# Gated linear attention and a squared-ReLU FFN on one core: a hand-written order of all work items is replaced by another order

## The chip, the cores and the metric

The kernel runs on one NeuronCore of a Trainium2 chip. The metric is device time in microseconds of one execution of the program; a few executions are made, and their median is quoted. Everything that is said of single instructions comes from one further execution, which the hardware profiler recorded.

## The reference: what is computed

The inputs of the attention are q, k, v and a complex gate (a_re, a_im), each of shape 4 x 8 x 768 x 48 (batch, heads, sequence, head dimension), in float32. The two weights of the FFN, 384 x 2048 and 2048 x 384, are float64.

```python
mag = np.sqrt(a_re * a_re + a_im * a_im)
scale = np.minimum(mag, 0.999) / (mag + 1e-06)
a_re_n, a_im_n = (a_re * scale, a_im * scale)
for t in range(S):                              # S_re, S_im start at zero
    ar, ai = a_re_n[:, :, t, :, None], a_im_n[:, :, t, :, None]
    new_re = ar * S_re - ai * S_im
    new_im = ar * S_im + ai * S_re
    S_re, S_im = new_re + einsum('bhd,bhe->bhde', k[:, :, t], v[:, :, t]), new_im
    y[:, :, t] = einsum('bhd,bhde->bhe', q[:, :, t], S_re)
x = y.transpose(0, 2, 1, 3).reshape(3072, 384)
h = np.maximum(x @ w_in, 0.0)
out = (h * h @ w_out).astype(np.float32)
```

## The kernel before

**Tiling.** Each sequence of 768 steps is cut into 6 chunks of 128. Two chunks of two different sequences form a *group*, so there are 12 groups, each of 2 x 128 = 256 tokens. Groups 0 to 5 walk through the first two sequences, 6 to 11 through the other two. Inside a chunk the recurrence is turned into matrix products (scores, a mask, a product with the values); between chunks a state of 48 x 48 per head is carried. When a group's 256 tokens are there, the FFN is run on them.

**Work items.** The whole program is a string of tokens, `FRONT` (line 1162 on), which `follow` (line 1307) reads from left to right. A token is a letter, a group or block number, and a step; `work` (line 1273 on) names the function behind each letter. Each function issues its few instructions on the engines that it needs. The block runs under `tc.manual_schedule` for all five engines, so every engine executes its instructions in the order in which the tokens stand, and semaphores make it wait where data or a buffer is not there yet. Nothing else sets the order: moving a token moves its instructions on all of its engines, and nothing else.

The letters that matter here, with `g` a group:

- `l`, `i`: loads of the four inputs a_re, a_im, q, k into one single buffer `raw` (on SyncE's queue and, for the first three groups, partly on GpSimd's). `v`: loads of the values. `f`, `j`: the two parts of the load of a weight block, on SyncE and GpSimd (blocks 0 to 7 are of w_in, 8 to 15 of w_out; three buffers `words`). `U`, `S` (ScalarE), `D`, `A` (VectorE): decoding of float64 words into float32; after `A` a block can be used.
- `w`, `W`: the weights are read once more, in 32 pieces, and checked for range. `w` is the load into the one buffer `again` (on SyncE's queue), `W` two passes of ScalarE over it. As there is one buffer, a `w` waits until the `W` before it has been done.
- `p0.k`, `q0.k`, `p1.k`, `q1.k`, and `og.k` from group 2 on: the 31 steps that make a group's operands from the gates (p and q are the two chunks of groups 0 and 1, done apart). Steps 3, 7, 11, 13, 15 to 17, 19, 20 and 23 to 30 are VectorE's, step 21 (`last_heads`) is six transfers on SyncE's queue, the others are ScalarE's.
- `ag.k`, `bg.k`: the steps of the group's two chunks. 0 scores (TensorE), 1 and 3 transposes of the keys (TensorE), 2 and 4 their copies (ScalarE), 5 mask (VectorE), 6 products with the values (TensorE), 7 copy to the token tile x (ScalarE), 8 sums for the state (TensorE), 9 new state (VectorE). `gg` (that is `g0`, `g0.1`, `g1.0`, ...): two small transfers that fill the gaps of x.
- `F`, `H`: first product of the FFN (TensorE, into one of two PSUM buffers of the pool `ph`) and ReLU with square (ScalarE, two passes). A group has eight of each from group 2 on (`Fg.0` to `Fg.7`); for groups 0 and 1 they are per chunk (`F0.1.0` is half 1 of blocks, chunk 0).
- `T`, `E`: the second product of groups 0 and 1 and its eviction. From group 2 on the second product is computed by seven products `Z0` to `Z6` of half-size blocks instead of eight; `X`, `Y`, `Q` (VectorE) are the sums of halves of h that this needs, `R0` to `R6` (`outputs`, line 1132 on) evict and add. `Z1`, `Z3` and `Z5` go into one tile `o_ps` that takes a buffer of the same pool `ph` as the first product; `R1`, `R3` and `R5` read it. `Z0`, `Z2`, `Z4` and `Z6` take turns in another tile. `t0` to `t3` make sums of blocks of w_out. `s`: stores.
- `M`: masks and zeroed buffers at the start. `K`: the verdict on the ranges; it decides at the end whether a slow general path has to be run, which does not happen with these inputs.

From group 4 to group 10 the string repeats nearly the same pattern: eight `F` with their `H`, then `Z0` to `Z6` between the steps of the two chunks of the next group, with the next group's operand steps strewn in, and a pair `W`, `w` at eight to four places of each group, in which the next `w` stands directly behind the `W` that frees its buffer.

Of the kernel before, what the change touches and what calls it, by code (L numbers as in the profile page):

```python
# [426 lines left out]
def quotient_path(ctx, tc, feat, vtok, w_in, w_out, w1, w2, out, n_seq, count):  # L427
# [245 lines left out]
    def weights(i, step):  # L673
        if i in words_of:
# [457 lines left out]
    def outputs(i, r):  # L1132
# [30 lines left out]
        "l0.0.0 M4 M8 M6 l0.0.1 j1 j0 i0.1.0 i0.1.1 M0 p0.0 p0.2 p0.3 M7 p0.4 q0.0 p0.5 q0.3 "  # L1163
        "p0.7 q0.4 q0.5 q0.7 M2 M3 f1 p0.8 p0.9 p0.1 p0.10 p0.11 p0.12 q0.2 U1 q0.1 S1 q0.8 "
        "q0.9 f0 U0 q0.10 D1 p0.15 p0.23 p0.24 p0.25 D0 p0.16 A1 p0.22 S0 f2 l0.1.1 l0.1.0 "
        "p0.26 q0.11 p0.27 j3 j2 j4 p0.13 q0.6 p0.17 A0 f3 f4 v0.0 p0.6 M1 p0.14 v0.1 l1.2.0 M5 "
        "p0.18 p0.19 D2 q0.12 q0.15 p0.28 p0.20 q0.22 U2 S2 f5 A2 U4 S4 p0.29 a0.3 a0.4 q0.23 "
        "D4 p0.30 a0.1 a0.2 U3 S3 q0.24 A4 q0.25 D3 q0.16 q0.26 q0.13 q0.27 A3 q0.17 p0.21 j6 "
        "j5 j7 f6 i1.2.0 a0.8 a0.0 a0.5 a0.6 q0.14 q0.18 U5 U6 a0.7 S5 i1.2.1 D6 q0.19 q0.28 "
        "q0.20 D5 p1.0 S6 p1.3 p1.4 p1.6 q0.29 q0.30 p1.5 g0.0 l1.2.1 f7 F0.0.0 A6 p1.7 A5 a0.9 "  # L1170
        "p1.2 p1.1 p1.9 p1.8 U7 p1.10 q1.0 b0.3 p1.11 D7 p1.12 b0.4 q0.21 f8 b0.0 f9 p1.15 q1.3 "
        "p1.23 S7 b0.1 A7 p1.24 b0.5 p1.22 b0.2 H0.0.0 p1.25 D8 p1.16 F0.1.0 f10 b0.8 b0.6 U8 "
        "H0.1.0 b0.7 S8 q1.4 F0.3.0 p1.13 p1.26 q1.1 U9 H0.3.0 p1.14 p1.27 A8 p1.17 p1.18 D9 "
        "p1.19 p1.28 p1.20 p1.29 p1.30 F0.2.0 T0.0.0 g0.1 F0.3.1 H0.2.0 S9 q1.2 H0.3.1 q1.5 U10 "
# [12 lines left out]
        "H1.2.1 H1.3.1 o3.15 o3.23 o3.24 b2.5 o3.25 o3.16 T1.0.1 a2.3 T1.1.1 T1.2.1 a2.4 b2.6 "
        "a2.8 b2.7 s1.0 g2 T1.3.1 T1.4.1 T1.5.1 T1.6.1 F2.7 F2.0 o3.13 o3.14 a2.9 o3.26 o3.27 "
        "o3.17 o3.18 o3.19 o3.28 o3.20 o3.29 o3.30 H2.7 s0.0 l4 H2.0 b2.3 T1.7.1 F2.1 b2.4 o4.0 "
        "H2.1 v3 o3.21 F2.2 o4.3 o4.2 E1.1 H2.2 o4.4 o4.5 o4.7 o4.8 F2.3 b2.1 F2.5 H2.5 o4.9 "  # L1190
        "b2.2 a3.0 X2.1 Y2.1 a3.5 F2.6 b2.8 a3.6 b2.9 o4.1 H2.3 X2.3 o4.10 a3.7 F2.4 a3.1 a3.2 "
        "b3.0 a3.3 Z2.0 H2.6 H2.4 t1 Y2.3 o4.11 o4.12 a3.4 b3.5 X2.0 a3.8 b3.6 Z2.1 Y2.0 o4.15 "
        "X2.2 Q2.1 Y2.2 Z2.3 a3.9 t2 t3 o4.23 o4.24 Q2.3 b3.7 g3 s1.1 F3.1 o4.22 R2.0 H3.1 R2.3 "
        "Q2.0 o4.25 Q2.2 Z2.2 b3.3 F3.4 o4.6 W0 R2.2 Z2.4 Z2.5 b3.4 H3.4 F3.5 o4.16 R2.1 o4.13 "
        "o4.14 o4.26 o4.27 o4.17 R2.5 v4 l5 w1 o4.18 H3.5 R2.4 o4.19 o4.28 F3.2 b3.1 F3.0 b3.2 "
        "H3.0 X3.0 o4.20 o4.29 o4.30 Z2.6 b3.8 b3.9 R2.6 H3.2 o5.6 F3.6 o4.21 X3.1 v5 s2.1 s2.0 "
        "o5.1 Y3.1 Y3.0 a4.1 F3.3 H3.6 X3.2 o5.2 Y3.2 F3.7 H3.3 a4.2 o5.0 a4.0 o5.3 H3.7 X3.3 "
        "o5.4 a4.3 Z3.0 a4.4 a4.5 o5.5 Y3.3 o5.7 a4.8 W1 w2 R3.0 a4.6 a4.9 o5.10 Z3.1 a4.7 o5.8 "
        "o5.9 Z3.2 R3.1 Q3.2 Q3.1 Q3.0 Q3.3 o5.11 b4.0 R3.2 b4.1 b4.5 o5.12 Z3.3 o5.22 o5.15 "
        "o5.23 o5.24 o5.25 b4.2 b4.6 W2 w3 R3.3 b4.3 b4.7 Z3.4 b4.4 g4 o5.13 b4.8 R3.4 o5.14 "  # L1200
        "Z3.5 v6 b4.9 l6 o5.16 o5.26 o5.27 W3 w4 F4.0 Z3.6 H4.0 R3.5 o5.17 F4.4 R3.6 o5.18 s3.0 "
        "o5.19 s3.1 F4.1 H4.4 F4.5 H4.1 X4.0 o5.20 o5.28 o5.29 o5.30 W4 w5 F4.2 H4.5 o6.6 F4.6 "
        "H4.2 X4.1 o5.21 Y4.1 o6.1 Y4.0 F4.3 H4.6 X4.2 o6.2 F4.7 Y4.2 H4.3 o6.0 a5.0 o6.3 H4.7 "
        "X4.3 o6.4 Z4.0 o6.5 a5.5 Y4.3 o6.7 a5.6 W5 w6 R4.0 Z4.1 a5.7 o6.10 o6.8 Z4.2 R4.1 Q4.2 "
        "o6.9 Q4.1 Q4.0 Q4.3 o6.11 b5.0 R4.2 Z4.3 b5.5 o6.12 o6.22 o6.15 o6.23 o6.24 o6.25 b5.6 "
        "W6 w7 R4.3 Z4.4 b5.7 v7 g5 o6.13 Z4.5 R4.4 o6.14 o6.16 o6.26 o6.27 Z4.6 l7 W7 w8 F5.0 "
        "R4.5 R4.6 o6.17 F5.4 H5.0 o6.18 o6.19 F5.1 H5.4 s4.0 s4.1 F5.5 H5.1 X5.0 o6.20 o6.28 "
        "o6.29 o6.30 W8 w9 F5.2 H5.5 o7.6 F5.6 X5.1 o6.21 H5.2 Y5.1 Y5.0 o7.1 a6.1 F5.3 H5.6 "
        "X5.2 o7.2 F5.7 Y5.2 H5.3 a6.2 a6.0 H5.7 X5.3 o7.0 a6.3 Z5.0 a6.5 a6.4 Y5.3 o7.3 a6.8 "
        "W9 w10 R5.0 o7.4 a6.6 a6.9 o7.5 Z5.1 a6.7 o7.7 o7.10 Z5.2 R5.1 Q5.2 o7.8 Q5.1 Q5.0 "  # L1210
        "Q5.3 o7.9 b6.0 o7.11 R5.2 b6.1 Z5.3 b6.2 b6.5 o7.12 b6.3 Z5.4 b6.4 o7.15 o7.23 o7.24 "
        "o7.25 W10 w11 R5.3 o7.22 b6.6 b6.8 b6.7 g6 R5.4 Z5.5 o7.13 v8 Z5.6 b6.9 o7.14 R5.5 "
        "o7.16 o7.26 o7.27 s5.0 W11 w12 F6.0 R5.6 l8 o7.17 F6.4 H6.0 F6.1 H6.4 X6.0 o7.18 Y6.0 "
        "s5.1 F6.5 o7.19 H6.1 W12 w13 F6.2 H6.5 X6.1 F6.6 H6.2 Y6.1 o7.20 o7.28 o7.29 o7.30 "
        "o8.6 F6.3 H6.6 o8.0 X6.2 o7.21 Y6.2 a7.1 o8.3 H6.3 F6.7 o8.1 Z6.0 H6.7 X6.3 o8.2 Y6.3 "
        "a7.0 W13 w14 R6.0 o8.4 a7.2 o8.5 a7.3 a7.5 Z6.1 a7.4 o8.7 Z6.2 R6.1 o8.10 Q6.2 Q6.1 "
        "o8.8 Q6.0 Q6.3 o8.9 a7.8 a7.6 a7.9 R6.2 Z6.3 a7.7 o8.11 b7.0 W14 w15 R6.3 o8.12 b7.1 "
        "b7.5 o8.22 Z6.4 o8.15 o8.23 o8.24 o8.25 b7.2 b7.6 b7.3 b7.7 Z6.5 b7.4 g7 R6.4 o8.13 "
        "b7.8 R6.5 o8.14 Z6.6 v9 b7.9 s6.0 l9 o8.16 o8.26 o8.27 W15 w16 F7.0 R6.6 F7.4 H7.0 "
        "o8.17 F7.1 H7.4 X7.0 o8.18 s6.1 Y7.0 F7.5 o8.19 H7.1 W16 w17 F7.2 H7.5 X7.1 F7.6 H7.2 "  # L1220
        "Y7.1 o8.20 o8.28 o8.29 o8.30 o9.6 F7.3 H7.6 o9.0 X7.2 o8.21 Y7.2 a8.1 o9.3 H7.3 F7.7 "
        "o9.1 Z7.0 H7.7 X7.3 o9.2 Y7.3 a8.0 W17 w18 R7.0 o9.4 a8.2 o9.5 a8.3 a8.5 Z7.1 a8.4 "
        "o9.7 Z7.2 R7.1 o9.10 Q7.2 Q7.1 o9.8 Q7.0 Q7.3 o9.9 a8.8 a8.6 a8.9 R7.2 Z7.3 a8.7 o9.11 "
        "b8.0 W18 w19 R7.3 o9.12 b8.1 b8.5 o9.22 Z7.4 o9.15 o9.23 o9.24 o9.25 b8.2 b8.6 b8.3 "
        "b8.7 Z7.5 b8.4 g8 R7.4 o9.13 b8.8 R7.5 o9.14 Z7.6 v10 b8.9 s7.0 l10 o9.16 o9.26 o9.27 "
        "W19 w20 F8.0 R7.6 F8.4 H8.0 o9.17 F8.1 H8.4 X8.0 o9.18 s7.1 Y8.0 F8.5 o9.19 H8.1 W20 "
        "w21 F8.2 H8.5 X8.1 F8.6 H8.2 Y8.1 o9.20 o9.28 o9.29 o9.30 o10.6 F8.3 H8.6 o10.0 X8.2 "
        "o9.21 Y8.2 a9.1 o10.3 H8.3 F8.7 o10.1 Z8.0 H8.7 X8.3 o10.2 Y8.3 a9.0 W21 w22 R8.0 "
        "o10.4 a9.2 o10.5 a9.3 a9.5 Z8.1 a9.4 o10.7 Z8.2 R8.1 o10.10 Q8.2 Q8.1 o10.8 Q8.0 Q8.3 "
# [141 lines left out]
```

## Time and profile before

| | us |
|---|---|
| three executions | 688.64, 689.97, 691.25 (median 689.97) |
| profiled execution, its own time | 688.9 |
| its span, first to last instruction | 687.1 |
| TensorE (PE) busy | 624.4 |
| TensorE's weight loads (beside the matmuls) | 552.9 |
| VectorE (DVE) busy | 498.9 |
| ScalarE (ACT) busy | 423.7 |
| GpSimd (POOL) busy | 35.4 |
| moved by DMA | 60.37 MB |

The page first gives each engine's busy time, then the span in 40 slices of 17.2 us, one digit a slice, in tenths. A group of instructions is named by line, engine and operation; many VectorE instructions come from one helper and so bear its line, 482. A wait is put down to the instruction that ended it. A matmul's end in the trace is modelled, so the distance from one start to the next is the better measure of what a matmul costs.

Since every engine follows the tokens in order, the trace can be read token by token: the instructions of an engine, counted off, fall to the tokens of the string. Times such as "R2.1 at 228.2" in the prediction are read in this way, in us from the start of the span.

### The profile page before, as it was taken

The numbers are of one execution on the slowest core, as the hardware profiler recorded it, in microseconds if no ns is written. First come the engines' busy times: TensorE is split into PE (matmuls) and PEld (weight loads), VectorE is DVE, ScalarE is ACT, GpSimd is POOL, SyncE is SP. The second block draws the span as 40 slices with busy tenths as digits, with TensorE's granted clock in tenths as the row PEclk, the third lists the DMA queues.
The fourth block names the chain that finished last, engine by engine and source line by source line (L and its number), as shares of the span: only waits on it lengthen the run. The fifth ranks groups of instructions, "written<-read, shape, count | busy, mean of one in ns | idle before, by whom it ended". The sixth has DMA issues, their size and how long they took to land.

```text
span 687.1 us, 13164 instructions
## 1 busy us (share of the span) xinstructions
PE 624.4 (91%) x5147; PEld 552.9 (80%) x5147; DVE 498.9 (73%) x973; ACT 423.7 (62%) x822; POOL 35.4 (5%) x82
## 2 busy tenths in 40 slices
PE   0058999999999699999999999989999999999996
PEld 0047987776889589989989999879979879989896
DVE  7989899969678668967858868858957966862130
ACT  6758997575674276496496585495486577451330
POOL 5250030000000000000000000000000000000000
PEclk9999999999999899999999999999999999999999
DMA  8987582441701341741731730730731531121101
GB/s 190 180 170 199 134 191 75 74 80 34 135 2 42 72 94 43 141 96 48 150 75 37 151 85 28 160 73 25 141 78 43 128 86 48 52 57 36 30 2 28
DMA packets 49232, 60.37 MB, mean 88 GB/s; under 512 B 6792, under 2 KB 40072, under 8 KB 49160
## 3 DMA queue, kind: packets, MB, share of 16 engines
q1 hardware_dynamic: 46336, 53.78, 35.4%
q0 software_dynamic: 2336, 5.21, 4.0%
q8 instruction: 42, 0.69, 0.4%
q10 hardware_dynamic: 488, 0.44, 0.2%
q14 instruction: 30, 0.25, 0.1%
HBM read 48.76 MB, written 4.72 MB: 78 GB/s over the span
## 4 chain that ended last, share of the span: by engine, by line
PE 69%; DMA 11%; DVE 8%; ACT 6%; SPq 3%; issue 1%; ACTq 0%; DVEq 0%
PE o_ps L1128 26%; PE h_ps L1038 22%; DMA raw<-in_feat_dram 8%; PE a_ps L921 6%; PE y L947 3%; PE h_ps L1022 3%; PE y L913 3%; PE add L969 2%; PE tp L928 2%; PE o_ps L1058 2%; DVE qk L482 2%; DMA again<-in_moe_w_out_dram 2%; DMA last<-qk 1%; DVE pr L482 1%; SPq L517 1%
## 5 line engine op out<-in xcount | busy, mean ns | idle before, releaser
L1038 PE MATMUL h_ps<-x,w 128*128 128x256 f32 x960 | 214.8, 382 | 10.8 <-DVE o L1004 5.9
L1038 PEld LDWEIGHTS h_ps<-x,w 128*128 128x128 f32 x960 | 181.9, 191 | 37.3 <-ACT h L1045 6.5
L1128 PE MATMUL o_ps<-w,h 128*128 128x192 f32 x640 | 111.1, 328 | 0.0
L1128 PEld LDWEIGHTS o_ps<-w,h 128*128 128x128 f32 x640 | 103.7, 190 | 1.9 <-issue 0.9
L1045 ACT ACTIVATE h<-h_ps 128x512 f32<-128x512 f32 x80 | 47.7, 597 | 61.7 <-PE h_ps L1038 60.2
L482 DVE TENSOR_TENSOR pr<-ab 128x384 f32<-128x384 f32 (+3 forms) x196 | 70.1, 375 | 3.9
L482 DVE TENSOR_TENSOR mix<-h 128x256 f32<-128x256 f32 x40 | 16.9, 423 | 62.9 <-ACT h L1046 62.8
L1128 PE MATMUL o_ps<-w_sum,mix 128*128 128x192 f32 x320 | 55.7, 328 | 0.0
L1022 PEld LDWEIGHTS h_ps<-x,w 128*128 128x128 f32 x384 | 47.9, 205 | 7.5 <-ACT room L750 3.5
L482 DVE TENSOR_TENSOR ab<-pr 128x48 f32<-128x48 f32 (+3 forms) x210 | 49.9, 260 | 5.3
L1022 PE MATMUL h_ps<-x,w 128*128 128x128 f32 x384 | 48.9, 289 | 4.9 <-DMA x<-x 3.1
L1128 PEld LDWEIGHTS o_ps<-w_sum,mix 128*128 128x128 f32 x320 | 52.1, 190 | 1.0 <-DVE state L482 0.7
L482 DVE TENSOR_TENSOR a<-a_ps,mask 128x1024 f32<-128x1024 f32 x24 | 29.3, 1223 | 31.5 <-PE a_ps L921 31.5
L1046 ACT ACTIVATE h<-h 128x512 f32<-128x512 f32 x80 | 50.5, 631 | 2.6
L482 DVE TENSOR_TENSOR qk<-ab,qk 128x768 f32<-128x768 f32 (+1 forms) x56 | 46.1, 842 | 1.1
L1058 PE MATMUL o_ps<-w,h 128*128 128x384 f32 x128 | 44.8, 491 | 0.0
L1001 ACT ACTIVATE o<-o_ps 128x192 f32<-128x192 f32 (+1 forms) x44 | 15.2, 345 | 45.6 <-PE o_ps L1128 45.1
L735 ACT ACTIVATE qk<-raw 128x768 f32<-128x768 f32 (+1 forms) x28 | 37.2, 1337 | 7.9 <-DVE raw L482 7.5
L921 PE MATMUL a_ps<-qk 48*128 48x128 f32 x576 | 39.9, 287 | 0.0
L482 DVE TENSOR_TENSOR room<-ab,carry 128x1344 f32<-128x1344 f32 (+1 forms) x28 | 36.7, 1352 | 3.1 <-ACT carry L851 3.0
L921 PEld LDWEIGHTS a_ps<-qk 48*128 48x128 f32 x576 | 35.2, 193 | 4.4 <-issue 4.3
L735 ACT ACTIVATE room<-z 128x768 f32<-128x768 f32 (+1 forms) x28 | 35.5, 1362 | 4.0 <-DVE z L782 4.0
(105 smaller groups left out, 892.5 us busy)
## 6 DMA issues: line engine op xcount, KB each, us to landing
raw<-in_feat_dram SPq DMA_DIRECT2D x40, 288.0 KB
words<-in_moe_w_out_dram SPq DMA_DIRECT2D x8, 768.0 KB
again<-in_moe_w_in_dram SPq DMA_DIRECT2D x16, 384.0 KB
again<-in_moe_w_out_dram SPq DMA_DIRECT2D x16, 384.0 KB
vt<-in_vtok_dram SPq DMA_DIRECT2D x24, 192.0 KB
out_dram<-o SPq DMA_DIRECT2D x23, 192.0 KB
last<-qk SPq DMA_DIRECT2D x60, 64.5 KB
raw<-in_feat_dram SPq DMA_DIRECT2D x120, 32.0 KB
```

What stands on the lines that cost most here:

```text
L482: nc.vector.tensor_tensor(out=out, in0=in0, in1=in1, op=op)
L735: nc.scalar.activation(out=out.rearrange("p c j n -> p c n j"), func=AF.Copy, in_=in_.rearrange("p c (n j) -> p c n j", j=L), **kwargs)
L913: nc.tensor.matmul(ys[p_ % 2][crossed(hh, p_), p_ // 2], lhsT=states[b][1 - c_seq % 2][rows(hh), c, p_], rhs=operand(c, p_, rows(hh)), sta ...
L921: nc.tensor.matmul(ps[:, hh, p_], lhsT=operand(2 + c, p_, rows(hh)), rhs=operand(c, p_, rows(hh)), start=(c == RE), stop=(c == IM))
L947: nc.tensor.matmul(tiles["y"][p_ % 2][crossed(hh, p_), p_ // 2], lhsT=v[:, at:at + ROWS], rhs=tiles["am"][:, hh, p_], start=(first and p_ ...
L1001: nc.scalar.activation(out=out, in_=x, func=AF.Copy, scale=of_w2)
L1022: nc.tensor.matmul(ps[:, j], lhsT=w1_blocks[:, k, g, at:at + P], rhs=x_of[i][:, g, b * C:(b + 1) * C], start=(g == 0), stop=(g == NG - 1))
L1038: nc.tensor.matmul(ps[:, j], lhsT=w1_blocks[:, k, g, at:at + P], rhs=x_of[i][:, g], start=(g == 0), stop=(g == NG - 1))
L1045: nc.scalar.activation(out=h, in_=h_ps[i, f], func=AF.Relu, scale=of_w1)
L1046: nc.scalar.activation(out=h, in_=h, func=AF.Square)
L1058: nc.tensor.matmul(o_of[i, b], lhsT=tokens_of(i, f, b)[:, j], rhs=w2[:, k], start=(k == 0), stop=(k == NFB - 1))
L1128: nc.tensor.matmul(to, lhsT=x(k)[:, j], rhs=factor(z)[:, 2 * k + j], start=(z in (0, 1, 3) and k == j == 0), stop=(k == KH // 2 - 1 and j ...
```

## The change

Only the string `FRONT` is another, and `sum_weights` asks for two sums by `get`, so that `t3` can be placed ahead of `t1` and `t2`. No instruction is added, taken away or given another shape; the sums on every engine are the same. The tokens of one group are in another order, the tokens of neighbouring groups are interleaved differently, and the pieces of the second reading of the weights come in an irregular order (`w7`, `w6`, `w8`, `w4`, `w9`, ...), from group 6 on with the `w` often just a few tokens ahead of its `W`. The diff, cut to four stretches: the start, the stretch in which group 2's second product ends, one later group, and the end.

```diff
@@ sum_weights
-        x, y = ((half[0][1], half[0][0]), (half[1][1], w2_sums[0] if i else None),
-                (half[1][0], w2_sums[1] if i > 1 else None), (half[1][1], half[0][1]))[i]
+        x, y = ((half[0][1], half[0][0]), (half[1][1], w2_sums.get(0)),
+                (half[1][0], w2_sums.get(1)), (half[1][1], half[0][1]))[i]
...
@@ FRONT
-        "l0.0.0 M4 M8 M6 l0.0.1 j1 j0 i0.1.0 i0.1.1 M0 p0.0 p0.2 p0.3 M7 p0.4 q0.0 p0.5 q0.3 "
-        "p0.7 q0.4 q0.5 q0.7 M2 M3 f1 p0.8 p0.9 p0.1 p0.10 p0.11 p0.12 q0.2 U1 q0.1 S1 q0.8 "
-        "q0.9 f0 U0 q0.10 D1 p0.15 p0.23 p0.24 p0.25 D0 p0.16 A1 p0.22 S0 f2 l0.1.1 l0.1.0 "
-        "p0.26 q0.11 p0.27 j3 j2 j4 p0.13 q0.6 p0.17 A0 f3 f4 v0.0 p0.6 M1 p0.14 v0.1 l1.2.0 M5 "
-        "p0.18 p0.19 D2 q0.12 q0.15 p0.28 p0.20 q0.22 U2 S2 f5 A2 U4 S4 p0.29 a0.3 a0.4 q0.23 "
-        "D4 p0.30 a0.1 a0.2 U3 S3 q0.24 A4 q0.25 D3 q0.16 q0.26 q0.13 q0.27 A3 q0.17 p0.21 j6 "
...
-        "X2.2 Q2.1 Y2.2 Z2.3 a3.9 t2 t3 o4.23 o4.24 Q2.3 b3.7 g3 s1.1 F3.1 o4.22 R2.0 H3.1 R2.3 "
-        "Q2.0 o4.25 Q2.2 Z2.2 b3.3 F3.4 o4.6 W0 R2.2 Z2.4 Z2.5 b3.4 H3.4 F3.5 o4.16 R2.1 o4.13 "
-        "o4.14 o4.26 o4.27 o4.17 R2.5 v4 l5 w1 o4.18 H3.5 R2.4 o4.19 o4.28 F3.2 b3.1 F3.0 b3.2 "
...
-        "b7.8 R6.5 o8.14 Z6.6 v9 b7.9 s6.0 l9 o8.16 o8.26 o8.27 W15 w16 F7.0 R6.6 F7.4 H7.0 "
-        "o8.17 F7.1 H7.4 X7.0 o8.18 s6.1 Y7.0 F7.5 o8.19 H7.1 W16 w17 F7.2 H7.5 X7.1 F7.6 H7.2 "
...
-        "Q10.0 Q10.3 a11.6 R10.2 Z10.3 a11.7 b11.0 W30 w31 R10.3 Z10.4 b11.5 b11.6 R10.4 Z10.5 "
-        "b11.7 g11 Z10.6 R10.5 s10.0 W31 F11.0 R10.6 s10.1 F11.4 H11.0 F11.1 H11.4 X11.0 K0 "
-        "Y11.0 F11.5 K1 H11.1 F11.2 H11.5 X11.1 Y11.1 F11.6 H11.2 F11.3 H11.6 X11.2 K2 Y11.2 "
...
+        "M7 M8 l0.0.0 M4 M2 M3 l0.0.1 M0 M1 p0.0 p0.2 p0.3 p0.4 p0.5 p0.7 q0.0 M6 q0.3 p0.9 "
+        "p0.8 p0.1 q0.4 p0.10 q0.5 p0.11 l0.1.0 f0 q0.7 i0.1.1 j0 i0.1.0 j1 j2 p0.12 p0.22 q0.8 "
+        "q0.10 U0 q0.1 q0.9 q0.2 S0 f1 U1 S1 p0.15 p0.23 D0 p0.24 p0.13 p0.25 q0.11 p0.16 A0 "
+        "p0.26 D1 f2 l0.1.1 f3 p0.27 M5 A1 p0.17 q0.22 p0.6 q0.13 p0.14 q0.12 q0.15 U2 p0.18 "
+        "q0.14 S2 p0.19 q0.23 D2 l1.2.0 f4 i1.2.0 j4 j3 j5 q0.24 p0.28 q0.25 p0.20 q0.16 p0.29 "
+        "q0.26 p0.30 q0.27 q0.17 a0.3 p0.21 a0.4 q0.6 i1.2.1 a0.1 p1.6 U3 q0.18 A2 U4 a0.2 S3 "
...
+        "a3.4 o4.11 o4.12 R2.0 R2.3 b3.5 o4.22 Z2.2 a3.1 b3.6 R2.2 a3.2 b3.7 a3.8 Q2.0 o4.15 t2 "
+        "o4.23 Q2.1 Z2.5 Z2.4 o4.13 a3.9 R2.5 R2.1 g3 w1 F3.3 o4.14 b3.1 H3.3 F3.7 H3.7 b3.2 l5 "
+        "s2.0 F3.2 o4.24 o4.25 R2.4 o4.16 o4.26 o4.27 b3.3 b3.4 o4.17 o4.18 o4.19 o4.20 o4.28 "
...
+        "o9.26 Q7.1 R7.4 o9.14 Z7.5 o9.27 o9.17 R7.5 o9.18 o9.19 w20 v10 g8 W20 F8.5 F8.1 l10 "
+        "w16 H8.5 F8.3 H8.1 F8.4 Z7.6 o9.28 b8.9 o9.20 H8.3 o10.0 o10.3 o9.29 o9.30 o10.6 W16 "
...
+        "o11.30 b10.1 F10.5 H10.5 F10.1 b10.2 H10.1 b10.3 F10.7 H10.7 b10.4 F10.3 H10.3 X10.1 "
+        "Y10.1 o11.21 s9.1 w23 W23 w28 a11.0 Z10.0 R10.0 a11.5 X10.3 Y10.3 Z10.1 X10.2 X10.0 "
+        "Y10.2 a11.6 b10.8 a11.7 W28 R10.1 Y10.0 Z10.2 b10.9 b11.0 Q10.2 Z10.3 Q10.1 Q10.0 "
+        "Q10.3 b11.5 b11.6 w27 R10.2 W27 w26 W26 b11.7 R10.3 Z10.4 Z10.5 R10.4 R10.5 w24 g11 "
+        "F11.2 W24 w25 W25 H11.2 Z10.6 F11.0 H11.0 w30 F11.4 H11.4 F11.1 H11.1 R10.6 F11.3 "
...
```

## The prediction

> **What bounds the kernel now.** I read the page's slices first, then what TensorE waits for, then the stretches in which it stands still.
>
> ```profile
> span 687.1 us, 13164 instructions
> ...
> PE   0058999999999699999999999989999999999996
> ...
> DVE  7989899969678668967858868858957966862130
> ...
> PEclk9999999999999899999999999999999999999999
> ```
>
> From the fourth slice on TensorE is full, but for a dip in slice 14 and the last slice. VectorE is as full as TensorE up to about 140 us and slack behind that. So two things set the end: when TensorE's dense stretch begins, and what it loses inside.
>
> How much it loses, I get from what each piece costs when it runs dense. The chain of waits gives it, since there the pieces follow each other without a gap:
>
> ```profile
> 641.69 10.36 PE h_ps L1038 x48
> ...
> 662.73 18.21 PE o_ps L1128 x112
> ```
>
> That is 10.36 / 4 = 2.59 us an `F` and 18.21 / 7 = 2.60 a `Z`. With the other chain pieces: 80 F x 2.59 = 207.2, 70 Z x 2.60 = 182.0, 16 half F x 2.69 = 43.0, 32 T x 1.29 = 41.3, 24 scores x 1.99 = 47.8, 20 state products x 1.03 = 20.6, 24 value products x 1.02 = 24.5, 20 state sums x 1.07 = 21.4, 40 transposes x 0.33 = 13.2: 601.0 us of work in both kernels. The span has 687.1, so 86 us are lost. Counting off the matmuls' starts at these prices: 51 us are lost before 60 us, 8 from 60 to 220, 8 from 220 to 240, 12 from 240 to 640, and 6 after the last matmul at 680.9 (eviction and store, the same in both). A new order can win only from these.
>
> ```profile
> PE h_ps L1038 <- DVE o L1004: 5.9, 1, 5.9
> PE h_ps L1038 <- ACT h L1045: 4.9, 4, 1.7
> ```
>
> These are the waits inside the dense stretch that an order can cure. The first is this, on VectorE's and TensorE's timelines:
>
> ```profile
> 228.17 0.36 DVE L1004 SCALAR_TENSOR_TENSOR o<-o_ps,o 128x192 f32<-128x192 f32 x1 [6.40 <-PE o_ps L1128]
> ...
> 236.18 0.61 DVE L1004 SCALAR_TENSOR_TENSOR o<-o_ps,o 128x192 f32<-128x192 f32 x2
> ```
> ```profile
> 236.59 4.54 PE L1038 MATMUL h_ps<-x,w 128*128 128x256 f32 x12 [5.92 <-DVE o L1004]
> ```
>
> `R2.1` needs `Z2.1`, which ended at 212.2, but it began at 228.17, just when `Z2.5` ended: both write the one tile `o_ps`, `Z2.5` stands ahead of `R2.1`, and the wait is for the tile. VectorE stood 6.4 us, then did `o4.13` to `o4.17` (8 us), and only then `R2.5`. The tile's `ph` buffer was not free for `F3.2` until then.
>
> **The change part by part.**
>
> *Group 2's eviction.* The new order has `Z2.5 Z2.4 o4.13 a3.9 R2.5 R2.1`, so VectorE has nothing queued between the last product and the two adds that free the buffer. The next to need it is now `F3.7`. Is it in time? From the end of `a3.0` VectorE has 10.3 us to `b3.5`, which waits for `b3.0`, 10.7 us later on TensorE; from there 10.6 us of its own work (11.2 at the 5% that instruction gaps add) to the end of `R2.1`: 22.0 us. TensorE has 23.7 us of work from `a3.0` to `F3.7`. So 1.7 us to spare and no wait. The wait's price is more than its length:
>
> ```profile
> 232.00:236.00 4.00, 0.00 (x0) 0.00 (x0) 3.65 (x17) 0.73 (x1) 0.00 (x0) 0.65 0.49 115
> 236.00:240.00 4.00, 3.41 (x8) 2.79 (x9) 3.97 (x7) 1.96 (x7) 0.00 (x0) 0.50 1.07 172
> ```
>
> The clock column (third from the end) falls to 0.50 after the stop, and `F3.2` took 4.54 instead of 2.59. Gain 5.92 + 1.95 = 7.9; I take 7.5, as some small wait will come into this place.
>
> *The second reading of the weights.* Three of the four waits on ACT h have this form in the chain:
>
> ```profile
> 442.36 0.53 ACT h L1046
> 442.88 3.72 DMA again<-in_moe_w_out_dram
> 446.60 0.02 issue
> ```
>
> `W16` stands ahead of `H7.5` on ScalarE, its load was issued late (SyncE was busy with the ten microseconds of `l9`), and ScalarE stood; then both `ph` buffers were full and TensorE waited at `F7.6`, `F8.6`, `F9.6`: 1.7, 1.4 and 1.3 us, 4.4 in all. In the new order a load of this kind has 3 us and more of ScalarE work between it and its `W` in groups 5 to 9 (after `w16`: three `H`, `o10.0`, `o10.6`). `W13` alone has only 1, but no `F` is due behind it. So all 4.4 go.
>
> New is a chain at the end: `W28`, `W27`, `W26`, `W24`, `W25` stand nearly side by side on ScalarE, and with one buffer each load waits for the pass before. A cycle is 3.72 us from issue to data by the row above, and 1.38 for the pass (446.62 to 448.00): 5.1 us. `W28` can begin when `a11.7` is done, 4.6 us after `Z10.0`; four cycles and a pass later, at 26.4, `W25` ends, and the first half of `H11.2` at 27.0. TensorE has 27.0 us of work from `Z10.0` to `F11.4`, which needs that buffer: just in time. `R10.3`, queued behind `W26`, ends at 17.3 where `Z10.5` wants to start at 16.6: 0.7 late. Here the Trainium skill ("DMA: Bandwidth & Descriptors", section "Anatomy of one DMA — SWDGE (gpsimd) path") would have 2.0 us fixed plus bytes at 436 GB/s, 0.9 for these 384 KB, so a cycle of 4.3 and no stall at all. The page's fit is for another queue and the trace shows 3.5 to 3.9 at three places, so I keep the row. Bounds: 0 by the page, 4 if a cycle is 6 us. I take 1.
>
> *The irregular middle.* Groups 4 to 10 are dense in both orders. I compared, dependency by dependency, the work ahead of producer and consumer; most slacks are 0.5 to 3 us where the old pattern had more. `F8.6` has 1 us behind `W16`, `a5.0` about 1 behind its transfer `o5.21`. Bounds 0 to 6 for what such places lose; 2 taken.
>
> *The front.* The work that VectorE has to do before `F0.2.0` can start (up to `A5`) grows from 48.8 to 55.5 us, since the loads of q and k come ahead of the weights and chunk 1's steps ahead of the decoding. `A5` ended at 57.3, that is 8.5 behind its sum; at the same delay it would be at 64.0. The new order delays VectorE more: `q0.11` now waits for `q0.1`, `q0.9`, `q0.2`, which stand behind `U0` on ScalarE, and `q0.19` for `q0.18` behind `U3`, whose load `j3` is behind `i1.2.0` on GpSimd's queue; about 2.5 together. So `F0.2.0` at 66.5. Then `b0.8`, `b0.6`, `F0.0.0`, `F0.3.0` to 76.7, `F0.3.1` waits 0.9 for `H0.0.0` on ScalarE, and `F0.1.1` starts at 80.3. Before it started at 78.9 with `T0.0.0` (1.3) done as well, so 77.6 for the same work: 2.7 lost. The first scores, at 45 us before, come later too (their transfer `p0.21` waits for `p0.30`, 35.2 before, 41 now), but `F0.1.0` at about 60 isn't held by them alone. One rule speaks against this part: the Trainium skill ("TensorE: Matmul & The Clock Gate", "Part 1: The HAM clock gate") has the clock halved after an idle window of 3.4 us, until a busy one has passed, as the two windows above show it. TensorE has a gap ahead of `F0.2.0`. By the rule alone I would add 1.7 us; but `F0.0.0` took 5.46 us for its 24 matmuls before (53.1 to 58.6, twice the price), so the first `F` runs slow in both, 60 to 65.3, and the gap is then 1.2: nothing added. Bounds -2 (no added delay on VectorE) to +9.
>
> *Sum*: 2.7 - 7.5 - 4.4 + 1 + 2 = -6.2. The span of 687.1 becomes 680.9. The profiled execution took 688.9, 1.8 more than its span, and lies 1.1 under the median of 689.97; I apply the difference to the median: **683.8 us**.
>
> **Rivals.** *The front slips (slower).* VectorE is full to 140 us, and the plan behind has its weights decoded just in time (`T0.7.0` wants `A15` within a microsecond). If `j3`, behind `i1.2.0` on GpSimd's queue, lands not at about 39 but at 50, ScalarE stands at `U3`, which all of chunk 1's steps follow, and the front loses 10 in place of 2.7. It decides from a front loss of 8.9 on. For it: the DMA share is 0.87 to 0.96 up to 40 us; against it: fewer weights are in flight by then. Time 690 + 1 = 691 at that price, 694 with 2 to 4 us of lost slack behind it.
>
> *The reloads and tight slacks eat it (no change).* A cycle of 6 us puts 4 us on the end, and tight places lose 4 instead of 2: -6.2 + 3 + 2 = -1.2, 688.8. Against it: no load was seen to take over 3.9.
>
> *More than I say (faster still).* VectorE's added delay in the front doesn't occur (0 in place of 2.7) and the middle loses nothing: -6.2 - 2.7 - 2 = -10.9, 679.1.
>
> *It only moves the wait.* `R2.5` is freed, but another late evict stops TensorE by 5 us: -1.2 again, counted with the second.
>
> **How the numbers follow.** Forecast 0.42, faster still 0.18, no change 0.21, front slips 0.19. A difference of 0.5%, 3.4 us, is about what a measurement of this kernel can tell from none. Of the forecast's 0.42, within 3 us of 683.8, some 0.36 lies below 686.5; with the 0.18: faster 0.55. Same: 0.06 + the no-change case's 0.19 = 0.25. Slower: 0.20. The range goes from 676 (the faster case less 3) to 695 (the front at its bound); the forecast's own range is 681 to 687.
>
> **What would show it.** Right: no wait of `h_ps` on `o L1004` over 2 us and no clock under 1 in the middle; `F0.1.1` near 80; VectorE's gap ahead of `R2.1` gone; ScalarE's waits for `again` bunched in the last 110 us, at about 3.5 each, with TensorE's loss there under 2. Wrong: TensorE's first dense stretch later than 84, VectorE gaps over 2 us before 60; waits of `h_ps` on ACT or DMA spread over groups 5 to 10; or `Z` held by `R` anywhere for microseconds.

## The result, and the profile after

| | before | after |
|---|---|---|
| median of the executions, us | 689.31 (4, from 686.42 to 691.25) | 670.91 (4, from 669.41 to 671.83) |
| ratio to before | | 0.9734, interval 0.9695 to 0.9774 |
| span of the profiled execution, us | 687.1 | 670.0 |

The new order is 2.7% faster, 18.4 us, and the profiled spans differ by 17.1. The prediction had the sign and 6.2 us of it; 670.9 lies below its range. (The four executions of the kernel before are the three given above and one more.)

The page of the kernel after, its span and three rows of its 40 slices (now of 16.75 us each):

```profile
span 670.0 us, 13180 instructions
...
PE   0058999999999999999999999999999999999996
...
DVE  7998996967979868959849958978948957753030
...
PEclk9997999999999999999999999999999999999998
```

TensorE's dip in slice 14 is gone. The clock's row has a new 7 in slice 4, in the front. What TensorE still waits for (us in total, times, longest one):

```profile
PE tp L928 <- DVE qk L482: 31.3, 1, 31.3
PE a_ps L921 <- DMA last<-qk: 6.7, 2, 3.5
PE turned L557 <- ACT mask L554: 5.1, 1, 5.1
PE o_ps L1058 <- DVE w L482: 1.6, 1, 1.6
```

The rest come to 0.8 us and less each. The first three stand before 58 us, the fourth at 110. Both waits of `h_ps L1038` that the prediction showed, for VectorE's `o` and for ScalarE's `h`, are missing, and the largest group of matmuls on the page has next to no idle time ahead of it (10.8 us before):

```profile
L1038 PE MATMUL h_ps<-x,w 128*128 128x256 f32 x960 | 212.3, 380 | 0.1
```

To see where the 17.1 us came from, I take for each product its end, less all TensorE work in front of it in its own order at the prediction's dense prices. This *lateness* grows where TensorE loses time, and it can be compared between orders:

| up to the end of | before | after | gained since the row above |
|---|---|---|---|
| `F0.1.1` (the front) | 54.5 | 52.9 | 1.6 |
| `Z2.5` (groups 0 to 2) | 59.2 | 57.8 | -0.2 |
| `a4.0` (group 2's eviction, group 3) | 67.2 | 57.8 | 8.0 |
| `b7.0` | 69.3 | 59.4 | 0.5 |
| `a10.0` (groups 7, 8, 9 of the FFN) | 77.7 | 60.8 | 7.0 |
| `Z11.6` (the last product) | 79.4 | 62.3 | 0.2 |

Two places hold 15.0 of the 17.1 us, and both are named in the prediction. Here is the first of them after the change, TensorE's timeline and then VectorE's (start, duration, engine, line, operation, number, and in brackets an idle time before it, of which there is none):

```profile
217.79 3.41 PE L1128 MATMUL o_ps<-w,h 128*128 128x192 f32 x20
221.04 2.75 PE L1038 MATMUL h_ps<-x,w 128*128 128x256 f32 x12
223.63 0.49 PE L928 MATMUL tp<-ident,qk 128*128 128x128 f32 x3
223.96 5.35 PE L1038 MATMUL h_ps<-x,w 128*128 128x256 f32 x24
```
```profile
220.37 0.56 DVE L482 TENSOR_TENSOR state<-pr 128x384 f32<-128x384 f32 x1
220.84 0.62 DVE L1004 SCALAR_TENSOR_TENSOR o<-o_ps,o 128x192 f32<-128x192 f32 x2
221.38 0.55 DVE L482 TENSOR_TENSOR pr<-ab 128x384 f32<-128x384 f32 x1
```

`R2.5` and `R2.1` are the two at 220.84, behind `a3.9` and with no gap. `F3.7`, which the prediction named as the first to need their buffer, starts at 223.96, 2.5 us later (1.7 forecast). The windows that had the halved clock before (PE busy, weight loads, DVE, ACT, POOL, then clock, DMA share, GB/s):

```profile
232.00:236.00 4.00, 4.00 (x21) 3.54 (x20) 3.93 (x4) 1.28 (x3) 0.00 (x0) 1.00 0.02 6
236.00:240.00 4.00, 4.00 (x20) 3.54 (x19) 2.96 (x4) 1.57 (x4) 0.00 (x0) 1.00 0.00 0
```

TensorE is busy in all of both, at full clock.

### The profile page after: what moved, and what is told of

It is laid out like the page before. It is cut to its first block, busy times and chain, and to the rows that moved or that the text cites. A ratio compares the mean times of both kernels' runs of the same rounds, so it can differ in the third digit from the quotient of the medians.

```text
span 670.0 us, 13180 instructions
## 1 busy us (share of the span) xinstructions
PE 617.4 (92%) x5147; PEld 552.3 (82%) x5147; DVE 496.4 (74%) x973; ACT 421.7 (63%) x822; POOL 35.3 (5%) x82
## 4 chain that ended last, share of the span: by engine, by line
PE 86%; DMA 6%; DVE 2%; SPq 2%; issue 1%; ACT 1%; POOL 0%; ACTq 0%; POOLq 0%
PE h_ps L1038 31%; PE o_ps L1128 28%; PE a_ps L921 6%; PE h_ps L1022 5%; PE o_ps L1058 5%; PE y L947 3%; PE y L913 3%; PE add L969 3%; DMA raw<-in_feat_dram 2%; DMA words<-in_moe_w_in_dram 2%; PE tp L928 2%; DMA last<-qk 1%; SPq L879 1%; DMA words<-in_moe_w_out_dram 1%; SPq L669 1%
## 5 line engine op out<-in xcount | busy, mean ns | idle before, releaser
L1038 PE MATMUL h_ps<-x,w 128*128 128x256 f32 x960 | 212.3, 380 | 0.1
L1038 PEld LDWEIGHTS h_ps<-x,w 128*128 128x128 f32 x960 | 181.1, 190 | 25.0 <-issue 0.4
L1128 PE MATMUL o_ps<-w_sum,mix 128*128 128x192 f32 x320 | 55.5, 328 | 0.0
L928 PE MATMUL tp<-ident,qk 128*128 128x128 f32 x120 | 21.8, 294 | 32.0 <-DVE qk L482 31.3
L1022 PEld LDWEIGHTS h_ps<-x,w 128*128 128x128 f32 x384 | 45.7, 198 | 1.7 <-ACT h L1028 0.2
L1022 PE MATMUL h_ps<-x,w 128*128 128x128 f32 x384 | 46.4, 281 | 0.0
L928 PEld LDWEIGHTS tp<-ident,qk 128*128 128x128 f32 x120 | 15.2, 148 | 36.6 <-issue 32.5
## 6 DMA issues: line engine op xcount, KB each, us to landing
last<-qk SPq DMA_DIRECT2D x60, 64.5 KB
```

The source lines that it names most:

```text
L928: nc.tensor.transpose(tp[:, g], qk_of[gi % 2][:, 2 + c, b, g, 0:C], ident)
L1022: nc.tensor.matmul(ps[:, j], lhsT=w1_blocks[:, k, g, at:at + P], rhs=x_of[i][:, g, b * C:(b + 1) * C], start=(g == 0), stop=(g == NG - 1))
L1038: nc.tensor.matmul(ps[:, j], lhsT=w1_blocks[:, k, g, at:at + P], rhs=x_of[i][:, g], start=(g == 0), stop=(g == NG - 1))
L1128: nc.tensor.matmul(to, lhsT=x(k)[:, j], rhs=factor(z)[:, 2 * k + j], start=(z in (0, 1, 3) and k == j == 0), stop=(k == KH // 2 - 1 and j ...
```

## The experiments

All are moves of tokens in `FRONT`: first five edits of the kernel before, then two mixtures of the orders, then three edits of the new order. Each time is a median, and behind it stands the ratio to executions of the kernel before that were made in between, with its 95% interval.

**The late `R2.5` alone.** Is it that one add, behind four other VectorE steps, that stops TensorE?

```diff
-... F3.5 o4.16 R2.1 o4.13 o4.14 o4.26 o4.27 o4.17 R2.5 v4 l5 w1 o4.18 H3.5 R2.4 ...
+... F3.5 o4.16 R2.1 R2.5 o4.13 o4.14 o4.26 o4.27 o4.17 v4 l5 w1 o4.18 H3.5 R2.4 ...
```

> The kernel before with one token moved: R2.5 directly behind R2.1, so that the buffer of o_ps is freed at about 229 instead of 236.5. VectorE still stands until Z2.5 is done and does o4.13 to o4.17 only afterwards. Theory (TensorE's lost time adds up, wherever it is lost): F3.2 no longer waits, minus 7.8 us. Rival (the work that VectorE holds back is needed by others too): F3.0 waits for H3.5, which stands on ScalarE behind o4.18, which waits for o4.17 on VectorE; and the scores a4.0 wait for the transfer o4.21, issued at 249 as before. Then only 1 to 3.6 us are gained.

Measured: 686.50 us, 0.9968 (0.9945 to 0.9992). The wait for VectorE's `o` is gone, and another has come; from TensorE's and ScalarE's timelines of this kernel:

```profile
228.97 5.34 PE L1038 MATMUL h_ps<-x,w 128*128 128x256 f32 x24
234.15 0.49 PE L928 MATMUL tp<-ident,qk 128*128 128x128 f32 x3
238.99 4.54 PE L1038 MATMUL h_ps<-x,w 128*128 128x256 f32 x12 [4.34 <-ACT h L1045]
```
```profile
237.61 0.34 ACT L851 COPY carry<-ab 128x180 f32<-128x180 f32 x1 [3.53 <-DVE ab L482]
...
238.36 0.57 ACT L1045 ACTIVATE h<-h_ps 128x512 f32<-128x512 f32 x1
```

`F3.2` now follows `F3.5` at once, and `F3.0` waits 4.34 us for `H3.5`, then runs at the slow 4.54. `H3.5` (238.36) stands on ScalarE behind `o4.18` (237.61), which needs VectorE's `o4.17`. So the old order blocked *both* buffers of the first product behind the same VectorE steps: one by `R2.5`, the other by a ReLU. The rival was right: freeing one gives 1.6 us of the 8 (from the end of `Z2.5` to that of `a4.0`; by the ratio 2.2, interval 0.6 to 3.8).

**Both adds, and `o4.17` last.** Three of the steps go first, then both adds, and `o4.17`, which `o4.18` waits for, behind them.

```diff
-... F3.5 o4.16 R2.1 o4.13 o4.14 o4.26 o4.27 o4.17 R2.5 v4 l5 w1 o4.18 H3.5 R2.4 ...
+... F3.5 o4.16 o4.13 o4.14 o4.26 o4.27 R2.1 R2.5 o4.17 v4 l5 w1 o4.18 H3.5 R2.4 ...
```

> The kernel before with R2.1 and R2.5 next to each other and behind o4.27, so that VectorE works on while Z2.5 runs, and frees the buffer right after it. Both theories: F3.2 starts at once, o4.17 is done 4 us sooner than before, H3.5 and a4.0 are in time: minus 7 to 8 us against the kernel before, and no halved clock near 235 us.

Measured: 680.17 us, 0.9889 (0.9846 to 0.9932). Lateness goes from 57.1 at `Z2.5` to 57.3 at `a4.0`, where the old order went up by 8.0: moving two tokens takes away the whole price of this place. VectorE does the other steps while `Z2.5` runs, and stands 1.9 us ahead of `R2.1` instead of 6.4:

```profile
226.17 0.62 DVE L1004 SCALAR_TENSOR_TENSOR o<-o_ps,o 128x192 f32<-128x192 f32 x2 [1.91 <-PE o_ps L1128]
```

**The checks later.** In groups 7 to 9, `W16`, `W20` and `W24` and their next loads are moved behind two more ReLUs.

```diff
-... H7.1 W16 w17 F7.2 H7.5 X7.1 F7.6 H7.2 Y7.1 ...
+... H7.1 F7.2 H7.5 X7.1 F7.6 H7.2 W16 w17 Y7.1 ...      (groups 8 and 9 alike)
```

> The kernel before with W16 w17, W20 w21 and W24 w25 moved behind H7.2, H8.2 and H9.2. Theory (the pass over the second reading, in front of H on ScalarE, is what stops F7.6, F8.6 and F9.6, and each stop costs what the run of eight F loses in the trace: 2.3, 2.1 and 1.9 us): minus 6.2 us. As predicted before the result, by the wait alone: minus 4.4 us. Rival (ScalarE only stands a little later, since the load itself is late): under 2 us gained.

Measured: 685.78 us, 0.9944 (0.9925 to 0.9964), 3.9 us by the ratio. Lateness from `b7.0` to `a10.0` grows by 3.4 us, where it grew by 8.4 before and by 1.4 in the new order. Part of the stall came back, at a place that TensorE's timeline of this kernel shows in group 7:

```profile
461.99 0.61 PE L921 MATMUL a_ps<-last 48*128 48x128 f32 x8
463.22 0.55 PE L928 MATMUL tp<-ident,qk 128*128 128x128 f32 x3 [0.62 <-ACT kt L933]
```

`a8.3`, a transpose, waits for `a8.2`, a copy on ScalarE. `W16` stands ahead of this copy in both orders. Counted from the end of `b7.0`, the copy begins only 1.6 us sooner than before, and TensorE could have been at `a8.3` 2.5 us sooner. The wait costs TensorE 0.85 us a group, from start to start.

**Both edits:** the second and the third experiment in one kernel.

> The kernel before with the edits of the second and third run together. If the gains add up: minus 13 to 14 us, that is three quarters of what the whole new order gains (17 us of span). Rival (the gained time is lost to the next wait): under 9 us.

Measured: 675.77 us, 0.9821 (0.9782 to 0.9860), 12.3 us by the ratio. The single edits gave 7.7 and 3.9, 11.6: they add up.

**The loads earlier.** Why was `w16` late at all? On SyncE's queue it stood behind `l9`, whose 16 transfers took 9.7 us to issue; of the kernel before, the first and the last of them and `w16`:

```profile
432.68 0.40 SPq L507 DMA_DIRECT2D raw<-in_feat_dram  x1
...
441.15 1.25 SPq L517 DMA_DIRECT2D raw<-in_feat_dram  x3
442.88 0.35 SPq L628 DMA_DIRECT2D again<-in_moe_w_out_dram  x1
```

This run leaves `W16` at its old place and puts its load ahead of `l9`, with `W15`, which frees the buffer. Group 2's eviction is as in the second experiment.

```diff
-... Z6.6 v9 b7.9 s6.0 l9 o8.16 o8.26 o8.27 W15 w16 F7.0 ...
+... Z6.6 v9 b7.9 s6.0 W15 w16 l9 o8.16 o8.26 o8.27 F7.0 ...      (l10, l11 alike)
```

> The kernel before with group 2's eviction put as in the run where R2.1 and R2.5 stand ahead of o4.17, and in groups 7 to 9 the pairs W15 w16, W19 w20 and W23 w24 moved four to nine tokens forward, so that they stand ahead of the loads l9, l10 and l11 on SyncE's queue (W16, W20 and W24 stay where they are). Theory (the load of w16 is late only because the ten microseconds of l9 stand ahead of it on SyncE, and moving W16 behind H7.2 only moved 0.85 us a group to the copy of a key that then stood behind it): all of the loss of groups 7 to 9 goes, 6.2 us, with the 7.8 of the eviction 14 us: 674 to 675 us, PE waits for neither ACT h nor ACT kt there, and the kernel comes to within 4 us of the new order from two local edits. Rival (these groups lose their time to something else in the old order, the loads l9 to l11 that come later now, or the steps strewn in between): no better than the 675.8 us of the two earlier edits together, over 2 us more at the start of group 10 than the new order has.

Measured: 674.43 us, 0.9767 (0.9741 to 0.9793), 15.7 us less than before. `w16` is now issued at 425.86, ahead of `l9`. The theory stands. ScalarE's timeline of this kernel at `W16`:

```profile
434.70 0.60 ACT L1045 ACTIVATE h<-h_ps 128x512 f32<-128x512 f32 x1 [0.60 <-PE h_ps L1038]
435.33 0.63 ACT L1046 ACTIVATE h<-h 128x512 f32<-128x512 f32 x1
435.87 0.55 ACT L636 ACTIVATE size<-again 128x384 bf16<-128x384 f32 x1
```

`W16` (the last line) starts without a wait, and the group of `F` matmuls has 0.2 us of idle time:

```profile
L1038 PE MATMUL h_ps<-x,w 128*128 128x256 f32 x960 | 211.9, 379 | 0.2 <-ACT h L1045 0.2
```

Lateness from `b7.0` to `a10.0` grows by 1.9 us. From the end of `a3.0` to the last product it grows by 6.8, in the new order by 5.0, in the old by 21.3. Two local edits of the old order so give 14.5 of the 16.3 us by which the new order beats it behind the front.

**The two halves of the new order.** One kernel has the new order's first 315 tokens (to `T0.1.1`) and then what is left in the old order:

> The first 315 tokens of the new order (to T0.1.1), then the rest in the old order. Theory (the new front is worth nothing by the end of it, since both kernels have lost the same 55.5 us at the end of b1.0): within 2 us of the kernel before. Rival (the new front brings the 2 us by which F0.1.1 is early, and more because loads and VectorE are better placed): 3 us or more faster.

The other has the old order's first 308 tokens (to `b1.5`) and then the rest in the new order:

> The first 308 tokens of the old order (to b1.5), then the rest in the new order. Theory: as fast as the changed kernel within 2 us, minus 15 to 18 us against the kernel before. Rival (the new rest needs the new front's loads): slower than the changed kernel by 4 us or more.

Measured: 692.90 us, 1.0053 (1.0026 to 1.0081), and 677.74 us, 0.9840 (0.9793 to 0.9888). Both lose at the seam: lateness at `b1.0` is 54.7 and 57.0, and at `a2.0` it is 60.0 and 62.8, a rise of 5.3 and 5.8 where the unmixed orders rise by 1.9 and 1.1. The one long wait there in the first of the two:

```profile
144.59 4.58 PE L1022 MATMUL h_ps<-x,w 128*128 128x128 f32 x24 [3.06 <-ACT h L1028]
```

It is `F1.2.1`. The ReLU ahead of it stood behind `o3.0`, which waited on ScalarE for its data. Such seams say nothing of either part by itself. What can be read is what lies beyond them: from `a2.0` to the end the kernel with the new rest goes from 62.8 to 68.0, up 5.2 (the new order: 5.4), and the one with the old rest from 60.0 to 82.7, up 22.7 (the old: 22.0). The gain is in the rest, whatever front is before it.

The front itself can be compared over all runs that have an unmixed start up to the end of `a3.0`. With the old front (before and five edits of it) lateness there is 58.1, 59.2, 56.1, 59.2, 56.7 and 59.2; with the new (after and the three edits below, one of which moves two tokens in it) 57.3, 56.9, 57.3 and 56.7. The means are 58.1 and 57.1: about 1.0 us gained, less than the old front's scatter of 3.

**The eviction undone in the new order.**

```diff
-... Z2.5 Z2.4 o4.13 a3.9 R2.5 R2.1 g3 w1 F3.3 ... F3.2 o4.24 o4.25 R2.4 o4.16 o4.26 o4.27 b3.3 b3.4 o4.17 o4.18 ...
+... Z2.5 Z2.4 R2.1 o4.13 a3.9 o4.24 o4.25 o4.16 o4.26 o4.27 o4.17 R2.5 g3 w1 F3.3 ... F3.2 R2.4 b3.3 b3.4 o4.18 ...
```

> The changed kernel with the eviction put back as before on VectorE alone: R2.1 ahead of o4.13, R2.5 behind o4.17; TensorE's order is the new one. Theory: VectorE stands until Z2.5 ends at about 218.6, R2.5 is done at 231.5, F3.7 waits 7 to 8 us from 224 on and then runs at half clock (plus 1 to 2 us): 8 to 10 us slower than the changed kernel. Rival (the new order has slack that takes it up): under 4 us slower.

Measured: 673.52 us, 0.9772 (0.9732 to 0.9811), some 2.6 us over the new order by the ratios, and not 8 to 10. TensorE's timeline of this kernel:

```profile
224.06 2.86 PE L1038 MATMUL h_ps<-x,w 128*128 128x256 f32 x12 [0.36 <-ACT h L1045]
227.60 2.86 PE L1038 MATMUL h_ps<-x,w 128*128 128x256 f32 x12 [0.69 <-ACT h L1045]
230.30 0.49 PE L928 MATMUL tp<-ident,qk 128*128 128x128 f32 x3
232.58 2.87 PE L1128 MATMUL o_ps<-w_sum,h 128*128 128x192 f32 x16 [1.79 <-DVE o L1004]
```

`R2.5` ran at 231.9, yet `F3.7` (224.06) and `F3.2` (227.60) each waited only for the ReLU just ahead: by these waits they took turns in the other buffer, and `H3.3` and `H3.7` were not behind `o4.18` on ScalarE. Then `Z2.6` waited 1.79 us for `R2.4`.

**The same, and the ReLUs behind `o4.18`.** If both buffers must be blocked for the full price, it should come back when the ReLUs are put behind `o4.18` as well.

```diff
-... o4.17 R2.5 g3 w1 F3.3 o4.14 b3.1 H3.3 F3.7 H3.7 ... b3.4 o4.18 o4.19 ...
+... o4.17 R2.5 o4.14 o4.18 g3 w1 F3.3 b3.1 H3.3 F3.7 H3.7 ... b3.4 o4.19 ...
```

> The new order with group 2's eviction as in the run before that undid it (R2.1 ahead of o4.13, R2.5 behind o4.17), and in addition o4.14 and o4.18 moved directly behind R2.5, so that ScalarE has o4.18, which needs VectorE's o4.17, ahead of H3.3 and H3.7 as the old order has it ahead of H3.5. Theory (in the old order two things held the two buffers at once, R2.5 the one and a ReLU behind o4.18 the other; undoing only R2.5 left F3.3, F3.7 and F3.2 the second buffer, so that it cost 3 us): now TensorE stops at F3.7 from about 224 to 232, 8 us, and the clock falls after it, 1.5 to 2 us more: 8 to 10 us over the new order, 679 to 681 us. Rival (the late R2.5 alone sets the price, and what it cost was 3 us): no more than 1 us over the 673.5 of the run before.

Measured: 680.90 us, 0.9869 (0.9836 to 0.9903); by the ratios 9.3 us over the new order and 6.7 over the run before. From this kernel's windows (columns as above), its TensorE and its ScalarE timeline:

```profile
228.00:232.00 4.00, 0.00 (x0) 0.00 (x0) 3.69 (x18) 0.13 (x1) 0.00 (x0) 0.53 1.14 171
232.00:236.00 4.00, 3.84 (x11) 3.21 (x12) 3.97 (x5) 1.83 (x7) 0.00 (x0) 0.61 0.40 71
```
```profile
223.05 0.49 PE L928 MATMUL tp<-ident,qk 128*128 128x128 f32 x3
232.16 6.89 PE L1038 MATMUL h_ps<-x,w 128*128 128x256 f32 x24 [8.61 <-DVE o L1004]
```
```profile
231.87 0.34 ACT L851 COPY carry<-ab 128x180 f32<-128x180 f32 x1 [9.17 <-DVE ab L482]
```

TensorE stands 8.61 us, and the two products behind the stop take 6.89 us for 5.2: 10.3 us lost, and `o4.18` begins on ScalarE only at 231.87. The old order's stop is rebuilt inside the new one.

**Two decoding steps earlier.** The last wait of the new order in its dense stretch is 1.6 us of `T0.7.0` for weight block 15.

```diff
 S15 moved to directly behind q1.21, A15 directly behind A14
```

> The changed kernel with S15 ahead of o2.0 and A15 ahead of o2.3, so that w_in's last block of the other matrix (block 15) is decoded at about 106 instead of 109.7 and T0.7.0 need not wait (1.6 us in the trace). Theory (lost time adds up): minus 1.6 us against the changed kernel. Rival (what follows is bound by the chain of o2 to o2.21 and a2.0, where TensorE waits 0.9 us in the trace, so that it is given back): within 0.8 us of the changed kernel.

Measured: 670.31 us, 0.9727 (0.9688 to 0.9765), no different from the new order. The wait is gone from the list, and lateness at `a2.0` is 56.9 in both. But the profile does not show what the edit did. In this execution TensorE was 1.4 us later already at `F0.1.1` (54.3 for 52.9), well ahead of the moved tokens, and 1.7 us later just before `T0.7.0`; by itself that takes the wait away. The run before this one has the two tokens at their old places, and there TensorE, as late, had no wait either. Only the time stands: the edit brought nothing that the executions show.

## Why the prediction was right or wrong

*Group 2's eviction: -7.5 forecast, -8.0 measured.* Right in place and size, for a reason that was half of it: the size came out because it was read off the stop as a whole, whatever held it. The prediction followed one buffer, from `R2.5` to `F3.2`; the second was blocked too, by `H3.5` behind `o4.18` behind `o4.17`. Moving `R2.5` alone gave 1.6 us, undoing it alone cost 2.6, and only both together cost 8 to 10. The new order cures both: the adds stand ahead of `o4.16` and `o4.17`, and the ReLUs `H3.3` and `H3.7` ahead of `o4.18`.

*The second reading of the weights: -4.4 forecast, -7.0 measured.* The mechanism was right, and it is shown by moving only `W15 w16` and the like ahead of `l9`, `l10` and `l11`, on top of the edit at group 2. The term of the sum was too small: the step added up what the list of waits gave, 1.7, 1.4 and 1.3 us. That list counts from the modelled end of the matmul ahead, which lies some 0.2 us behind the start of the next where they run dense. Counted from start to start, `F7.6`, `F8.6` and `F9.6` lost 1.9, 1.7 and 1.5 us. `a8.1`, `a9.1` and `a10.1` lost another 0.4 each, waiting for VectorE's `qk`, whose steps had stood behind an `X` that waited for the late ReLU. That is 6.4 in all, and these waits are gone with the loads moved. Some 0.6 more of the new order's gain is spread thinly over these groups.

*The front: +2.7 forecast, -1.6 measured in this pair of profiles, -0.8 over all.* This step failed: the delay of VectorE that it added did not take place, and `F0.2.0` did not have to wait for the whole of `A5`. Of the kernel after, TensorE's timeline in the front, VectorE's at `q0.11` and at the second half of `A5`, and ScalarE's at `q0.9` and `q0.2`:

```profile
57.11 1.19 PE L921 MATMUL a_ps<-last 48*128 48x128 f32 x6 [3.22 <-DMA last<-qk]
58.23 0.90 PE L928 MATMUL tp<-ident,qk 128*128 128x128 f32 x3
58.92 7.11 PE L1022 MATMUL h_ps<-x,w 128*128 128x128 f32 x48
```
```profile
19.30 0.55 DVE L802 SCALAR_TENSOR_TENSOR room<-room 128x384 f32<-128x384 f32 x1
...
63.19 0.95 DVE L482 CUSTOM_DVE_ANT_0 w<-w,part 128x1536 uint16<-128x1536 uint16 x1
```
```profile
17.65 0.85 ACT L735 ACTIVATE room<-z 128x384 f32<-128x384 f32 x1
18.31 0.85 ACT L735 ACTIVATE ab<-raw 128x384 f32<-128x384 f32 x1
```

`q0.11` starts at 19.30 with no gap, though the prediction had it wait for `q0.2`: that ended at 19.2. A sum of ScalarE's durations ahead of `q0.2` overstates its time, as neighbours there start 0.1 to 0.2 us before the one ahead has ended; how much of the 2.5 us this explains, the traces don't say. Nor did `U3` hold `q0.19`: it started at 39.60 without a wait, and `q0.18` behind it waited 0.28 us for VectorE. `A5` ended at 64.1, the 55.5 us of work and the same 8.5 us as before, so none of the 2.5 us of added delay took place. `F0.2.0` began at 63.2, before `A5`'s end, since only its later matmuls need that block: 3.3 us ahead of the forecast's 66.5. `F0.3.1` did not wait the 0.9 either, and `F0.1.1` began at 76.1 instead of 80.3, which is these 4.2 us. `F0.1.0` ran slowly, as forecast: 4.3 us to the next start for 2.7, with a granted clock of 0.50 and 0.72 in the two windows from 56 to 64 us. Most of this price was hidden: at full clock the later matmuls of `F0.2.0` would have come to stand until `A5`'s end at 64.1, and they started at 64.5. By these times I estimate 0.4 us lost of 1.6.

Of the 1.6 us in this pair, 1.2 come from the kernel before, whose `F0.1.0` took 3.8 us in this execution (granted clock 0.82 and 0.76 from 60 to 68 us) and 2.7 in its five edits. All seven profiles that begin with the old front have lateness 52.1 to 56.1 at `F0.1.1`, mean 54.1, and the five that begin with the new one 52.5 to 54.3, mean 53.3. So the forecast loss is not there, and a gain of about 0.8 lies within the scatter.

*The chain at the end: +1 forecast, 0 measured.* This step failed too, in the length of a cycle. ScalarE's waits for `again` in the kernel after, and the passes of `W28`, `W27`, `W26`, `W24` and `W25` on its timeline:

```profile
ACT size L636 <- DMA again<-in_moe_w_out_dram: 14.7, 6, 5.1
...
ACT size L636 <- DMA again<-in_moe_w_in_dram: 3.3, 2, 2.3
```
```profile
606.34 0.57 ACT L636 ACTIVATE size<-again 128x384 bf16<-128x384 f32 x1
...
610.58 0.55 ACT L636 ACTIVATE size<-again 128x384 bf16<-128x384 f32 x1 [0.53 <-DMA again<-in_moe_w_out_dram]
...
614.57 0.56 ACT L636 ACTIVATE size<-again 128x384 bf16<-128x384 f32 x1 [2.60 <-DMA again<-in_moe_w_out_dram]
...
618.53 0.55 ACT L636 ACTIVATE size<-again 128x384 bf16<-128x384 f32 x1 [1.29 <-DMA again<-in_moe_w_out_dram]
...
622.72 0.55 ACT L636 ACTIVATE size<-again 128x384 bf16<-128x384 f32 x1 [2.81 <-DMA again<-in_moe_w_out_dram]
```

From start to start a cycle is 4.0 to 4.2 us, not 5.1. Only the first of a `W`'s two passes reads `again`, so the next load is issued some 0.7 us after its start and not 1.38; the load itself took 3.3 to 3.6 us from issue to use. The Trainium skill's 4.3 ("DMA: Bandwidth & Descriptors", "Anatomy of one DMA — SWDGE (gpsimd) path"), which the prediction set aside, came nearer, but not for its own reason: its 2.9 us for the transfer is below all that was measured here, and the prediction's 1.38 for the pass was too much. (The trace of before has 3.4 to 3.9 us from issue to data at the three places where the prediction read 3.5 to 3.9.) `R10.3` and `F11.4` were in time. ScalarE stands 18.0 us for its loads of `again` in the new order and 11.4 in the old, and the new order loses none of it on TensorE.

*The irregular middle: +2 forecast, -0.5 (`a4.0` to `b7.0`) and -0.2 (behind `a10.0`) measured.* The allowance for tight slacks was not needed: none of the narrow places that were named lost more than 0.2 us.

*The rivals.* "More than I say" had the front's delay away and the middle lossless, and it was right in both; it still ended at 679.1, since it took both gains as fixed and kept 1 us for the end. "The front slips" hung on `j3` landing at 50 us; it landed at 38.1. "It only moves the wait" is what happens to half of the edit (the first experiment), but not to the whole order.

*The numbers.* Against the sum of -6.2, the spans' -17.1 is made up of 0.5 more at the eviction, 2.6 more at the loads, 4.3 at the front, and 3.5 where the forecast had put 1 + 2 for the end and the middle. All four point one way: three losses that did not take place and one gain read too small. The range allowed for larger losses at each step, but for no gain larger than forecast except in the front, so its lower end, 676, was too high.

## What to carry to other kernels

Where two buffers take turns, look for what holds each of them before you price the release of one: here one sat behind VectorE's queue, the other behind a ReLU that sat behind the same steps by way of ScalarE, and curing one gave a fifth of the gain. Take the price of a stop from start to start, over the stop, the products behind it and what the late results hold up elsewhere, and not from the list of waits alone. And before a whole order is replaced, try moving the few tokens at its two or three visible stalls: two such edits gave 15.7 us, where the whole new order gave 18.4.

## What the runs showed of the hardware that was not expected

A stop's aftermath did not grow with the stop. Before the change, TensorE stood 5.9 us, and the granted clock was 0.65, 0.50 and 1.00 in three windows of 4 us, which makes 6.8 us at half speed; when it stood 8.61 us, it was 0.53 and 0.61, 6.9 us. The wait of 3.06 us in the kernel with the new front and the old rest gave 0.70 and 0.87, 3.4 us of it. These are two and one of the 3.4 us windows that the Trainium skill describes ("TensorE: Matmul & The Clock Gate", "Part 1: The HAM clock gate"). But most of the longer spell passes while TensorE stands anyway: beyond the wait as listed, the three stops cost 1.95, 1.7 and 1.9 us.

The page puts the fall of the clock behind an idle window of about 3.4 us. Here a stop of 2.74 us, in the kernel with the old front and the new rest, was followed by 0.61 and 0.96 in two windows of 4 us, again 3.4 us at half speed; even from the start of the last matmul ahead of it TensorE was idle for only 3.0 us. The measurement decides. After the stop of 1.79 us above, the clock stayed at 1.00, and the stop cost 0.3 us beyond the wait as listed.

The old front is not equally fast each time. With the same tokens in the same order, lateness at the end of `a3.0` lay between 56.1 and 59.2 us in six profiled executions. Most of the spread is there by the end of `F0.1.0`, which came between 65.2 and 67.8 us. Ahead of it TensorE waited 6.7 to 8.7 us for small transfers (`last` and the gaps of x); whether these decide was not tried. It limits what one pair of profiles can say about the front to about 3 us.
